# Loading x0 on the ACT queue, with short reads of W1 ahead on the SP queue

## The chip, the cores and the metric

The kernel runs on one core of a Trainium2 chip. The metric is the device time of one execution in microseconds (us). The profile's span, from the first to the last instruction, is about 1.8 us shorter. All quoted runs are of the fast state, or of a kernel that was run once ("unknown"); every profiled run has a mean granted TensorE clock of 1.0 (the share of full clock that the chip allowed). Engines: PE is TensorE, PEld its weight loads, DVE VectorE, ACT ScalarE, POOL GpSimd, SP SyncE. A name ending in q is the engine's issue of transfers.

## The reference, cut to what matters

```python
# x: 1 x 2048 x 640;  W1: 640 x 1536;  bf16
xn = layernorm(x)
out = x + linear_attention(xn, wqkv, wo) + (gelu(xn @ W1 + b1) @ W2 + b2)
```

The argument is about the first 12 us: tile 0 of x (128 tokens, "x0") is loaded, normalised and transposed, and then multiplied with W1. Everything else in the kernel stays as it was.

## The kernel before

All loads of x and W1 are issued by SP, in this order. W1 is 640 x 1536 and comes in four pieces of 384 columns, 480 KB each; a tile of x is 160 KB.

```python
def dma_x(t, n):
    dma("sync", x_in[:, t:t + n, :], ...)
def dma_w1(i):                      # piece i: 384 columns, 5 x 384 elements per partition
    lo, hi = W1P[i]
    dma("sync", W1[:, :, lo:hi], w1v[:, :, lo:hi], [r_W1[i]])

dma_x(0, 1)
dma_x(1, 1)
dma_w1(0)
dma_w1(1)
dma_x(2, 1)
dma_x(3, 1)
dma_w1(2)
...
```

What runs until the first matmul with W1 (cut; `filler` issues dummy matmuls on constants, which keep PE busy until tile 0 is ready):

```python
dma(s_, b1tmp[:], ...)              # b1 on the ACT queue
filler(10)                          # 10 dummies of 512 columns
filler(6, P)                        # 6 of 128 columns
ln_half(0, 0); ln_half(0, 1); ln_aggr(0)      # statistics of tile 0
ln_half(1, 0); ln_half(1, 1)                  # statistics of tile 1
ln_norm(0)                                    # normalise tile 0
transp2(0, b, b + 1)                          # transpose on PE
...
copy2(0, b, b + 1)                            # PSUM to SBUF, ACT and DVE
# order of the first work on W1 ("T1", "T2": transposes of tiles 1 and 2)
plan = h_list(0, 1, 0, 3) + ["T1"] + h_list(0, 1, 3, 6) + h_list(1, 1, 0, 6) + h_list(0, 1, 6, 9)
plan += ["T2"] + ...
```

The first three units (15 matmuls) use W1 piece 0. What follows T1 (60 matmuls) begins with piece 1.

## Time and profile before

| | before |
|---|---|
| time, first 3 runs | 207.79 us (207.78 to 207.91) |
| time, all 39 runs of this study | 207.33 to 208.19 us |
| span of the profiled run | 205.9 us |
| x0 issued, landed | 0.81, 3.20 us |
| first W1 matmul | 6.86 us |
| W1 piece 1 landed | 7.94 us |

Landing times with two decimals are those of the last of a transfer's 16 parts in the trace's records of landings.

From the page of the kernel before, the busy time of PE (us, share of the span, number of instructions; the line goes on with the other engines), and the shares of the engines in the chain that ended last:

```profile
PE 202.7 (98%) x1639; PEld 140.2 (68%) x1639; DVE 109.6 (53%) x227; ACT 74.6 (36%) x153; POOL 35.1 (17%) x85
...
PE 98%; issue 0%; DVE 0%; ACT 0%
```

PE is the whole chain. The chain of waits in order of time (start in us, length in us, what):

```profile
0.84 5.07 PE ps L302 x16
5.91 0.33 PE ps L318 x3
...
6.86 1.00 PE ps L380 x15
...
8.13 3.38 PE ps L380 x60
11.51 0.28 PE ps L361 x5
```

L302 is the dummies, L318 the transposes of tiles 0 and 1, L380 the matmuls with W1, L361 the transposes of tile 2 (T2). The dummies run straight into tile 0's transposes; after 6.86 the chain holds nothing but PE.

From the timeline, SP's issues and DVE's first use of x0 (start, length, engine, line, operation; in brackets idle time and what ended it):

```profile
0.81 0.87 SPq L247 DMA_DIRECT2D xPK<-in_A_x_dram  x2
...
1.73 0.99 SPq L247 DMA_DIRECT2D W<-in_B_w_dram  x2
...
3.23 0.89 DVE L331 BATCH_NORM_STATS2 stats<-xPK 128x6 f32<-128x320 bf16 x2 [3.23 <-DMA xPK<-in_A_x_dram]
```

Each row with x2 is two issues: x0 and x1 from 0.81, W1 pieces 0 and 1 from 1.73. The view of the transfers gives for the issue in progress at 2.3 to 2.45 us, which is W1 piece 1 (number, size, us from issue to landing):

```profile
W<-in_B_w_dram SPq DMA_DIRECT2D x1, 480.0 KB, 5.7
```

Three stretches of time: bounds and length, then busy time of PE, PEld, DVE, ACT, POOL with instruction counts, granted clock, busy share of the DMA engines, and last the GB/s that they moved:

```profile
2.20:3.00 0.80, 0.80 (x4) 0.24 (x3) 0.00 (x0) 0.11 (x1) 0.00 (x0) 1.00 0.98 334
3.20:4.20 1.00, 1.00 (x3) 0.29 (x2) 0.89 (x2) 0.00 (x0) 0.23 (x1) 1.00 0.80 167
4.20:5.00 0.80, 0.80 (x3) 0.29 (x2) 0.78 (x3) 0.00 (x0) 0.49 (x1) 1.00 1.03 348
```

The last column is what to read. While x0 and x1 move it is 334 GB/s; when W1 begins it falls to 167 for a whole microsecond; then it is back at 348.

### The profile page before, as it was taken

The numbers are of one execution on the slowest core, as the hardware profiler recorded it, in microseconds if no ns is written. First come the engines' busy times: TensorE is split into PE (matmuls) and PEld (weight loads), VectorE is DVE, ScalarE is ACT, GpSimd is POOL, SyncE is SP. The second block draws the span as 40 slices with busy tenths as digits, with TensorE's granted clock in tenths as the row PEclk, the third lists the DMA queues.
The fourth block names the chain that finished last, engine by engine and source line by source line (L and its number), as shares of the span: only waits on it lengthen the run. The fifth ranks groups of instructions, "written<-read, shape, count | busy, mean of one in ns | idle before, by whom it ended". The sixth has DMA issues, their size and how long they took to land.

```text
span 205.9 us, 4084 instructions
## 1 busy us (share of the span) xinstructions
PE 202.7 (98%) x1639; PEld 140.2 (68%) x1639; DVE 109.6 (53%) x227; ACT 74.6 (36%) x153; POOL 35.1 (17%) x85
## 2 busy tenths in 40 slices
PE   8999999999999999999999999999999999999995
PEld 2999988544457777777746445677777777777775
DVE  3684288100007888999348888734864322523322
ACT  2699888666676555111153554300000000000000
POOL 3243065800000000999100200000000000000000
PEclk9999999999999999999999999999999999999999
DMA  5958845699910000000000000968611110010011
GB/s 163 348 161 100 241 114 113 132 375 322 360 39 3 0 0 3 0 0 0 3 0 0 2 3 16 357 190 164 159 65 61 36 34 32 33 35 32 32 39 60
DMA packets 24843, 19.70 MB, mean 96 GB/s; under 512 B 9976, under 2 KB 24824, under 8 KB 24824
## 3 DMA queue, kind: packets, MB, share of 16 engines
q1 hardware_dynamic: 23072, 17.86, 29.1%
q10 hardware_dynamic: 1752, 1.58, 4.0%
q8 instruction: 13, 0.21, 0.4%
q14 instruction: 6, 0.05, 0.1%
HBM read 13.11 MB, written 2.62 MB: 76 GB/s over the span
## 4 chain that ended last, share of the span: by engine, by line
PE 98%; issue 0%; DVE 0%; ACT 0%
PE ps L672 36%; PE ps L380 26%; PE ps L489 11%; PE ps L514 11%; PE ps L555 10%; PE ps L302 2%; PE ps L609 1%; PE ps L565 1%; PE ps L619 1%; PE ps L318 0%; DVE W L723 0%; PE ps L361 0%; PE ps L538 0%; ACT b1c L310 0%; ACT xnT L326 0%
## 5 line engine op out<-in xcount | busy, mean ns | idle before, releaser
L672 PE MATMUL ps<-W,HG 128*128 128x320 bf16 (+2 forms) x396 | 54.8, 295 | 0.0
L380 PE MATMUL ps<-xnT,W 128*128 128x128 bf16 (+2 forms) x505 | 53.0, 267 | 0.1
L380 PEld LDWEIGHTS ps<-xnT,W 128*128 128x128 bf16 x505 | 38.4, 98 | 14.1 <-issue 0.3
L672 PEld LDWEIGHTS ps<-W,HG 128*128 128x128 bf16 x396 | 38.1, 98 | 14.5 <-ACT Msb L591 0.2
L384 ACT ACTIVATE HG<-ps,b1c 128x128 bf16<-128x128 f32 (+2 forms) x101 | 42.4, 463 | 11.3 <-PE ps L380 9.3
L683 DVE TENSOR_TENSOR W<-ps,xnT 128x640 bf16<-128x640 f32 x15 | 12.4, 824 | 35.8 <-PE ps L672 34.7
L477 ACT ACTIVATE ek<-ps 128x512 bf16<-128x512 f32 (+1 forms) x36 | 23.2, 644 | 20.4 <-PE ps L555 10.3
L478 DVE TENSOR_SCALAR ek<-ek 128x512 bf16<-128x512 bf16 (+1 forms) x36 | 11.0, 305 | 32.5 <-ACT ek L477 31.3
L672 PE MATMUL ps<-Msb,PQ 128*128 128x320 bf16 (+2 forms) x165 | 24.2, 295 | 0.0
L555 PE MATMUL ps<-xnT,Wqkv 128*128 128x512 bf16 x100 | 21.9, 379 | 0.0
L489 PE MATMUL ps<-Wqkv,xnT 128*128 128x320 bf16 x160 | 21.9, 299 | 0.0
L514 PE MATMUL ps<-xPK,xn_tm 128*128 128x320 bf16 x160 | 21.9, 299 | 0.0
L672 PEld LDWEIGHTS ps<-Msb,PQ 128*128 128x128 bf16 x165 | 15.9, 98 | 5.9
L489 PEld LDWEIGHTS ps<-Wqkv,xnT 128*128 128x128 bf16 x160 | 15.7, 98 | 6.2
L514 PEld LDWEIGHTS ps<-xPK,xn_tm 128*128 128x128 bf16 x160 | 15.7, 98 | 6.1
L508 POOL COPY Wqkv<-Wqkv 128x128 bf16<-128x128 bf16 x25 | 15.1, 603 | 22.9 <-PE ps L489 21.4
L331 DVE BATCH_NORM_STATS2 stats<-xPK 128x6 f32<-128x320 bf16 x32 | 14.0, 477 | 9.3 <-DMA xPK<-in_A_x_dram 9.3
L555 PEld LDWEIGHTS ps<-xnT,Wqkv 128*128 128x128 bf16 x100 | 9.7, 98 | 11.4
L480 DVE SCALAR_TENSOR_TENSOR PQ<-ps,ek 128x512 bf16<-128x512 f32 x20 | 13.8, 692 | 2.1
L480 DVE SCALAR_TENSOR_TENSOR xPK<-ps,ek 128x640 bf16<-128x640 f32 x16 | 13.2, 824 | 1.7
L526 DVE TENSOR_TENSOR Msb<-Msb,xPK 128x640 f32<-128x640 f32 x14 | 11.6, 825 | 0.5
L341 POOL TENSOR_TENSOR rstd<-aggr,mhalf 128x1 f32<-128x1 f32 x16 | 9.9, 620 | 9.0 <-DVE aggr L339 9.0
(57 smaller groups left out, 78.4 us busy)
## 6 DMA issues: line engine op xcount, KB each, us to landing
xnT<-in_A_x_dram SPq DMA_DIRECT2D x4, 640.0 KB, 6.2
Wqkv<-in_A_wqkv_dram SPq DMA_DIRECT2D x3, 800.0 KB, 7.9
out_dram<-W SPq DMA_DIRECT2D x15, 160.0 KB, 1.8
W<-in_B_w_dram SPq DMA_DIRECT2D x4, 480.0 KB, 6.1
W<-in_B_w_dram SPq DMA_DIRECT2D x1, 1920.0 KB, 12.2
xn_tm<-rden ACTq DMA_DIRECT2D x12, 128.0 KB, 3.4
xPK<-in_A_x_dram SPq DMA_DIRECT2D x4, 320.0 KB, 5.3
Wo<-in_A_wo_dram SPq DMA_DIRECT2D x8, 160.0 KB, 8.8
```

Of the source, the lines that this page charges most:

```text
L331: Pl.ins(v, lambda e: e.bn_stats(stats[:, s, 6 * h:6 * h + 6], x_in[:, t, h * HW:(h + 1) * HW]), reads=r_x[t], writes=[r_stats[s][h]])
L380: Pl.ins(pe, [(lambda e, k=k: e.matmul(bank(b, 0, w), W1[:, k, jb * P:(jb + 1) * P], xnT[:, k, tok], start=(k == 0), stop=(k == DT - 1))) ...
L384: Pl.ins(s_, lambda e: e.activation(HG[:, jb, tok], bank(b, 0, w), ACT.Gelu_apprx_tanh, bias=b1c[:, jb:jb + 1]), reads=[B_[b], r_b1c], wri ...
L477: Pl.ins(s_, lambda e: e.activation(e2, src, ACT.Exp), reads=br, writes=[r_ek[s]])
L480: Pl.ins(v, lambda e: e.scalar_tensor_tensor(out=d2, in0=src, scalar=0.0, in1=e2, op0=ALU.max, op1=ALU.add), reads=br + [r_ek[s]], writes= ...
L489: fns.append(lambda e, k=k, h=h, b=b, t=t: e.matmul(bank(b + h, 0, HW), xnT[:, k, t * P:(t + 1) * P], Wqkv[:, k, D + h * HW:D + (h + 1) * ...
L508: Pl.ins(g, lambda e, k=k, i=i: e.tensor_copy(plain(Wqkv[:, k, D:2 * D], i), parts(Wqkv[:, k, 0:D], i)), reads=[r_Wq], writes=[r_Wk, r_WqP])
L514: Pl.ins(pe, [(lambda e, t=t, h=h, b=b, f=f, i=i: e.matmul(bank(b + h, 0, HW), xn_tm[:, t, f * P:(f + 1) * P], PK[:, t, h * HW:(h + 1) * H ...
L526: Pl.ins(v, lambda e, t=t: e.tensor_tensor(out=zsum, in0=zsum, in1=PK[:, t, :], op=ALU.add), reads=[r_PK[t], r_zsum], writes=[r_zsum])
L555: Pl.ins(pe, [(lambda e, k=k, j=j, b=b: e.matmul(bank(b), Wqkv[:, k, D + j * P:D + (j + 1) * P], xnT[:, k, cc], start=(k == 0), stop=(k == ...
L672: Pl.ins(pe, [(lambda e, i=i, x=x, bb=bb: e.matmul(bank(bb, 0, x[1] - x[0]), seq[i][0], seq[i][1][:, x[0]:x[1]], start=(i == 0), stop=(i = ...
L683: Pl.ins(v, lambda e: e.tensor_tensor(out=halves(out_sb[:, s, :]), in0=pair(b), in1=halves(x_res[:, t, :]), op=ALU.add), reads=B_[b:b + 2] ...
```

## The change

W1's start is slow. The intent, as read from the diff, is to touch W1 early with 80 reads of 32 bytes (16 partitions, 5 pieces each, spread over W1), and to move x0 to the other queue so that it doesn't wait behind them.

```diff
+        touch = sb("touch", [16, DT * 16], BF16)
...
-        def dma_x(t, n):
-            dma("sync", x_in[:, t:t + n, :], ...
+        def dma_x(t, n, eng="sync"):
+            dma(eng, x_in[:, t:t + n, :], ...
...
-        dma_x(0, 1)
+        dma("sync", touch[:].rearrange("p (k c) -> p k c", k=DT),
+            w1v.rearrange("(a b) k n -> a b k n", b=P // 16)[:, 0, :, 0:16], [R_("touch")])
+        dma_x(0, 1, s_)
         dma_x(1, 1)
         dma_w1(0)
         dma_w1(1)
```

No instruction of PE, DVE or POOL changes. ACT's table load and its load of b1 come after x0's issue.

More of the change, by code (lines that the diff above doesn't have):

```diff
@@ L250, in dma_t @@
             Pl.ins(eng, lambda e: e.dma_start_transpose(dst, src), reads=reads, writes=writes, dma=True)
-        def dma_x(t, n):
-            dma("sync", x_in[:, t:t + n, :], xv[t * P:(t + n) * P, :].rearrange("(t p) d -> p t d", p=P),
+        def dma_x(t, n, eng="sync"):
+            dma(eng, x_in[:, t:t + n, :], xv[t * P:(t + n) * P, :].rearrange("(t p) d -> p t d", p=P),
                 sum(r_x[t:t + n], []))
```

## The prediction

> **What bounds the kernel.** TensorE: the page gives PE 98% busy of a 205.9 us span at granted clock 1.0, and the chain of waits is PE from end to end. The list of waits has no wait of PE for a DMA; after its first W1 matmul at 6.86 us PE never idles. Only what moves that 6.86, or opens a gap after it, moves the time (207.79 us).
>
> **The start (timeline, 0 to 8 us).** SP issues x0 at 0.81; it lands 2.4 us later, at 3.2, and DVE's first statistics start (3.23). Then rstd on POOL (to 5.08) and normalisation of tile 0 from 5.20; its first part ends near 5.57. PE meanwhile runs 16 dummy matmuls from 0.84: ten of 512 columns, 0.43 us apart, six of 128, about 0.11 apart, so to about 5.7. The transposes start at 5.71. So dummies and tile 0 finish together: an earlier x0 gains nothing, a later x0 costs its delay nearly one for one. Then ACT copy 6.27 to 6.76, W1 matmuls at 6.86.
>
> **What the change aims at.** Windows of 0.2 us show 295 to 358 GB/s while x0 and x1 move (2.2 to 3.0), only 54, 108, 161, 230 GB/s from 3.2 to 4.0 when W1 begins, and over 330 from 4.2. Against 340 GB/s about 200 KB are missing, some 0.6 us. The 80 short reads over W1 seem meant to take this slow first contact early, with x0 on the ACT queue so as not to wait behind them.
>
> **What it is worth.** W1 piece 0 (issued 1.73, landing 4.7 us later) is there at 6.4, wanted at 6.86; piece 1 (2.2 + 5.7) at 7.9, wanted near 8.0; piece 2 (3.81 + 6.5) at 10.3, wanted near 10.5. All tight but in time: having them 0.3 to 0.6 us earlier gives PE nothing. Gain on the chain: about 0.
>
> **What it costs.**
> - SP issues the short reads in x0's slot, about 0.43 us either way; x1 and W1 keep their issue times within 0.1 us. x1 (landing 3.55, wanted 4.35) has 0.8 us to spare.
> - ACT issues x0 before its table load (1.28 us) and b1 (issue 0.62 us); both have over 2 us of slack. x0's issue comes 0 to 0.15 us later than SP's.
> - The Trainium skill, "DMA: Bandwidth & Descriptors", section "Issuing engines are not separate DMA queues", says transfers of different issuing engines interleave on the same 16 DMA engines; no run here shows it yet. So x0 shares with the short reads, which may hold an engine during their slow first contact, and with x1. I estimate x0 landing 0.1 to 0.6 us later (3.3 to 3.8 us).
>
> Sum: 0 gained, 0.05 to 0.5 us lost at the start, most likely near 0.15.
>
> **Prediction: 207.95 us, range 207.5 to 208.5; faster by over 2%: 0.01, within 2%: 0.98, slower by over 2%: 0.01.**
>
> **What would show it.**
> - The slow stretch at W1's start shrinks or moves ahead of x1; W1 piece 0 lands 0.2 to 0.6 us earlier.
> - DVE's first statistics start at 3.3 to 3.8; the first transpose and first W1 matmul come later by the same less about 0.05. The end moves by that alone.
> - PE still never waits for DMA after its first W1 matmul.
>
> **What would make it wrong.** If the dummies end earlier (PE reaches full clock at another moment), the start could gain 0.1 to 0.2 us. If the short reads hold x1 and W1 behind them, pieces 1 and 2, with 0.1 to 0.2 us of slack, become PE waits and the loss reaches 1 us. If x1 slips over 0.8 us, it delays tile 0's normalisation, which follows x1's statistics on DVE.

## The result

| | before | after |
|---|---|---|
| time, same rounds | 207.83 us (207.75 to 207.91, 6 runs) | 207.91 us (207.66 to 208.27, 6 runs) |
| ratio, after over before | | 1.0004, 95% interval 0.9991 to 1.0017 |
| once more, later | 207.65 us (207.43 to 207.83, 11 runs) | 207.53 us (207.43 to 207.90, 5 runs) |
| ratio | | 1.0001, interval 0.9988 to 1.0014 |

A ratio is the mean time of one kernel's fast runs over that of the other's of the same rounds, so it is not quite the ratio of the medians. The change does nothing that these runs can tell from zero.

The profile after, in the same views. The page's first line:

```profile
PE 203.0 (98%) x1639; PEld 140.1 (68%) x1639; DVE 109.6 (53%) x227; ACT 74.7 (36%) x153; POOL 35.1 (17%) x85
```

The chain of waits (three lines were added to the file, so L305, L321, L383, L364 are the dummies, the transposes of tiles 0 and 1, the W1 matmuls, and T2):

```profile
0.84 5.06 PE ps L305 x16
5.91 0.53 PE ps L321 x5
...
6.92 1.00 PE ps L383 x15
...
8.21 3.52 PE ps L383 x60
11.74 0.28 PE ps L364 x5
```

The timeline's issues, and DVE's first use of x0:

```profile
0.81 0.40 SPq L248 DMA_DIRECT2D touch<-in_B_w_dram  x1
...
0.82 0.42 ACTq L248 DMA_DIRECT2D xPK<-in_A_x_dram  x1
...
1.26 0.41 SPq L248 DMA_DIRECT2D xPK<-in_A_x_dram  x1
...
1.72 1.02 SPq L248 DMA_DIRECT2D W<-in_B_w_dram  x2
...
3.20 0.89 DVE L334 BATCH_NORM_STATS2 stats<-xPK 128x6 f32<-128x320 bf16 x2 [3.20 <-DMA xPK<-in_A_x_dram]
```

W1 piece 1, from issue to landing:

```profile
W<-in_B_w_dram SPq DMA_DIRECT2D x1, 480.0 KB, 6.0
```

The three stretches:

```profile
2.20:3.00 0.80, 0.80 (x4) 0.24 (x3) 0.00 (x0) 0.56 (x2) 0.00 (x0) 1.00 0.89 302
3.20:4.20 1.00, 1.00 (x3) 0.29 (x2) 0.89 (x3) 0.00 (x0) 0.23 (x1) 1.00 0.70 171
4.20:5.00 0.80, 0.80 (x3) 0.29 (x2) 0.80 (x3) 0.00 (x0) 0.52 (x1) 1.00 1.09 359
```

From the list of waits (who waited for what: us in total, times, longest), the one wait of PE's weight loads for W1:

```profile
PEld ps L383 <- DMA W<-in_B_w_dram: 0.2, 1, 0.2
```

The reader should see four things. x0 is not late: DVE starts on it at 3.20 against 3.23, although ACT issues it. The short reads take x0's slot on SP (0.40 us), so x1 and W1 keep their issue times (1.26, 1.72). The slow microsecond is still there, 171 GB/s against 167. And this trace is 0.23 us longer at T2 (11.74 against 11.51): 0.06 us at the first W1 matmul and the rest where PE waits at 8.21 for W1 piece 1, which landed at 8.17.

### One sum that fits every trace

A reading that all the experiments use, with their traces already in the table. The matmuls after T2 are the same in all kernels here, and PE does them without a gap that differs: span minus the start of T2 is between 194.4 and 194.5 us in all fourteen traces. So everything happens before T2, and there two things compete:

- from the first W1 matmul to T2 takes 4.63 us if nothing waits (6.90 to 11.53 in the run touch_wide below);
- from the landing of W1 piece 1 to T2 takes 3.57 us (8.17 to 11.74 in the trace after).

T2 starts at the later of the two:

| trace | x0 landed | first W1 matmul | W1 piece 1 landed | later of (matmul + 4.63, piece 1 + 3.57) | T2 measured | span |
|---|---|---|---|---|---|---|
| before | 3.20 | 6.86 | 7.94 | 11.51 | 11.51 | 205.9 |
| after | 3.17 | 6.92 | 8.17 | 11.74 | 11.74 | 206.2 |
| after_again | 3.18 | 6.62 | 7.76 | 11.33 | 11.33 | 205.8 |
| act_only | 3.79 | 7.24 | 7.44 | 11.87 | 11.87 | 206.3 |
| touch_only | 3.54 | 6.98 | 8.23 | 11.80 | 11.80 | 206.2 |
| touch_wide | 3.25 | 6.90 | 7.76 | 11.53 | 11.53 | 206.0 |
| spacer | 3.19 | 7.02 | 8.40 | 11.97 | 11.97 | 206.4 |
| wait_only | 3.08 | 6.57 | 7.73 | 11.30 | 11.29 | 205.7 |
| x1_act | 3.27 | 7.80 | 7.30 | 12.43 | 12.43 | 206.9 |
| eight_dummies | 3.26 | 6.70 | 7.67 | 11.33 | 11.32 | 205.8 |
| eight_again | 3.18 | 6.63 | 7.69 | 11.26 | 11.26 | 205.7 |
| after_eight | 3.15 | 6.76 | 7.86 | 11.43 | 11.43 | 205.9 |
| w2_touch | 3.30 | 6.92 | 8.31 | 11.88 | 11.88 | 206.3 |
| w2_split | 3.14 | 6.82 | 8.26 | 11.83 | 11.83 | 206.3 |

The two constants are read from touch_wide and after; the other twelve traces follow within 0.01 us. The sum is still a description. It is useful because it says for each run what set the time: what comes before the first W1 matmul (x0, x1, the dummies or piece 0), or W1 piece 1. In nine of the fourteen traces, the kernel before among them, it is piece 1 (in eight_again the two are equal).

### The profile page after: what moved, and what is told of

It is laid out like the page before. It is cut to its first block, busy times and chain, and to the rows that moved or that the text cites. A ratio compares the mean times of both kernels' runs of the same rounds, so it can differ in the third digit from the quotient of the medians.

```text
span 206.2 us, 4085 instructions
## 1 busy us (share of the span) xinstructions
PE 203.0 (98%) x1639; PEld 140.1 (68%) x1639; DVE 109.6 (53%) x227; ACT 74.7 (36%) x153; POOL 35.1 (17%) x85
## 4 chain that ended last, share of the span: by engine, by line
PE 98%; DVE 0%; issue 0%
PE ps L675 36%; PE ps L383 26%; PE ps L517 11%; PE ps L492 11%; PE ps L558 10%; PE ps L305 3%; PE ps L612 1%; PE ps L568 1%; PE ps L622 1%; PE ps L321 0%; DVE W L726 0%; PE ps L364 0%; PE ps L541 0%; PE ps L311 0%
## 5 line engine op out<-in xcount | busy, mean ns | idle before, releaser
L383 PE MATMUL ps<-xnT,W 128*128 128x128 bf16 (+2 forms) x505 | 53.0, 267 | 0.1
L383 PEld LDWEIGHTS ps<-xnT,W 128*128 128x128 bf16 x505 | 38.4, 98 | 14.2 <-DMA W<-in_B_w_dram 0.2
```

The lines of the kernel that those rows point to most:

```text
L383: Pl.ins(pe, [(lambda e, k=k: e.matmul(bank(b, 0, w), W1[:, k, jb * P:(jb + 1) * P], xnT[:, k, tok], start=(k == 0), stop=(k == DT - 1))) ...
```

## The experiments

Theories at the start. A: W1's slow microsecond is how a long load with several pieces per partition starts, so touching W1 can't help. B: it is first contact with W1's memory, and the short reads soften it. S came after the first four runs: the short reads are worth only the time for which they hold x1 back. C: what scatters is the moment at which PE reaches full clock, seen through the dummies.

### The two halves alone, and the change once more

act_only is the changed kernel without the short reads:

```diff
-        dma("sync", touch[:]..., w1v...[:, 0, :, 0:16], [R_("touch")])
         dma_x(0, 1, s_)
```

> Half of the change: x0 on the ACT queue, no short reads. SP then issues x1 at 0.81 us and W1 piece 0 at about 1.27, 0.45 us earlier than before. Theory A (the slow stretch at W1's start is how a long load with several pieces per partition starts, engine after engine): the stretch keeps its depth and its length of about 1 us but begins up to 0.4 us earlier, W1 piece 1 lands at 7.5 to 7.8 instead of 7.9 to 8.2, PE has no wait for W1, 207.7 to 207.8 us. Theory B (the stretch is first contact with W1's memory, and the short reads soften it): the stretch is deeper than with the short reads, and W1 lands no earlier than 7.9. In either case the time is within 0.15% of before, because x0 lands at 3.2 and PE's dummy matmuls run to 5.7.

Measured: 208.14 us (208.03 to 208.18, 5 runs), ratio to before 1.0023 (1.0011 to 1.0035). Both theories had said "within 0.15% of before, because x0 lands at 3.2", and both missed. Timeline and chain of this run:

```profile
0.81 0.40 SPq L247 DMA_DIRECT2D xPK<-in_A_x_dram  x1
...
0.82 0.41 ACTq L247 DMA_DIRECT2D xPK<-in_A_x_dram  x1
...
3.81 0.89 DVE L331 BATCH_NORM_STATS2 stats<-xPK 128x6 f32<-128x320 bf16 x2 [3.81 <-DMA xPK<-in_A_x_dram]
```

```profile
0.82 2.97 DMA xPK<-in_A_x_dram
...
6.22 0.36 PE ps L318 x3
...
7.24 1.00 PE ps L380 x15
...
11.87 0.28 PE ps L361 x5
```

x0 is issued as early as ever, but x1 is now issued in the same moment on the other queue. The trace's packets show the two interleaved: x1's first and last packet start at 1.83 and 3.18 us, x0's at 2.11 and 3.39; in the kernel before, x0's are at 1.85 and 2.59, and x1's follow from 2.59. So x0 lands at 3.79 instead of 3.20, the chain now begins with x0's transfer (2.97 us of it), and the first W1 matmul comes at 7.24. This agrees with the Trainium skill, "DMA: Bandwidth & Descriptors", section "Issuing engines are not separate DMA queues": transfers from different engines share the same 16 DMA engines and interleave. In return W1 landed early (piece 1 at 7.44), which bought nothing, as x0 was later still.

touch_only is the other half:

```diff
-        dma_x(0, 1, s_)
+        dma_x(0, 1)
```

> The other half: short reads first, x0 on SP behind them. Both theories: x0 is issued at 1.25 and lands at 3.6 instead of 3.2, x1 at 3.9 to 4.0, first transpose at 6.0 to 6.1 instead of 5.7, first W1 matmul at 7.1 to 7.2 instead of 6.86. W1 piece 0 is issued at 2.2 and lands 0.3 to 0.5 later (6.8 to 6.9), piece 1 at 8.3 to 8.6, close to its use at 8.3. Time 208.1 to 208.6 us. Were PE's start not set by x0, the time would stay at 207.8.

Measured: 207.93 us median; five runs from 207.74 to 207.96 and one of 210.04, which makes the ratio 1.003 (1.0001 to 1.0059). That run alone has a mean granted clock of 0.992; the other five average 207.89 us, 0.25 above before. The median is below the expected 208.1 to 208.6. x0 landed at 3.54, and the first W1 matmul came at 6.98, less late than expected. W1 piece 1 landed at 8.23 and set the time. In this half too x0's delay reaches the first W1 matmul, only smaller.

> The changed kernel once more, for a second trace and the scatter of its times. If the PE wait of 0.2 us for W1 piece 1 comes from the change, it is there again and piece 1 lands at 8.1 to 8.3; if it was chance (one DMA engine late), piece 1 lands anywhere from 7.8 to 8.3 and the time follows it. Median 207.7 to 208.0, spread again over 0.4 us, which is more than the 0.16 of before.

Measured: 207.53 us (207.43 to 207.90), ratio 1.0001. W1 piece 1 landed at 7.76 instead of 8.17 in the same program. So the wait of 0.2 us in the first trace need not come from the change. In the table, w2_touch and w2_split load x and W1 exactly as the kernel before does, and piece 1 landed at 8.31 and 8.26 there: the lateness is a lottery that both kernels play. The landing records show how: in the trace of before, 15 of the 16 parts of piece 0 landed between 5.17 and 5.76 us and the last at 6.46, and in piece 1 one part is 0.7 us behind again.

### Do the short reads prepare W1?

touch_wide reads 32 bytes of every row of W1, 640 reads instead of 80:

```diff
-        touch = sb("touch", [16, DT * 16], BF16)
+        touch = sb("touch", [P, DT * 16], BF16)
-            w1v.rearrange("(a b) k n -> a b k n", b=P // 16)[:, 0, :, 0:16], [R_("touch")])
+            w1v[:, :, 0:16], [R_("touch")])
```

> The short reads on all 128 partitions: 640 of 32 bytes, every row of W1[...]. Theory B (first contact with W1's memory, the 80 reads being too few or on the wrong engines): the slow stretch after x1 vanishes (over 250 GB/s in all windows of 0.2 us from 3.2 to 4.2) and W1 piece 1 lands at 7.6 or earlier. Theory A (start-up of a long load with several pieces per partition): the stretch stays, and the short reads, being such a load themselves, take 0.5 to 1 us more and delay x1 and W1 by as much; W1 piece 1 lands after 8.2, time 207.9 to 208.6.

Measured: 207.86 us (207.68 to 208.06), ratio 1.0012 (1.0000 to 1.0024). The microsecond from 3.2 stayed slow, at 145 GB/s, which speaks against B, though these reads landed only at 3.48, when W1 had already begun. x1 landed at 4.64 and held up tile 0's normalisation, which comes after x1's statistics on DVE. W1 piece 1 landed at 7.76: neither "7.6 or earlier" (B) nor "after 8.2" (A).

spacer turns the 80 short reads to Wqkv, which nothing needs before 40 us:

```diff
-            w1v.rearrange("(a b) k n -> a b k n", b=P // 16)[:, 0, :, 0:16], [R_("touch")])
+            wqv.rearrange("(a b) k n -> a b k n", b=P // 16)[:, 0, :, 0:16], [R_("touch")])
```

> The changed kernel with its 80 short reads turned to Wqkv, which nothing needs before 40 us: same shape, same place in SP's queue, no contact with W1. Theory S (the short reads are worth only the 0.45 us by which they hold back x1's issue, so that x0 has the DMA engines to itself): as the changed kernel: x0 lands at 3.1 to 3.3 against 3.8 with x0 on ACT and no short reads, W1 piece 1 at 7.7 to 8.3, time 0.2 to 0.6 us below that kernel's, 207.5 to 208.0. Theory B (they prepare W1's memory): W1 piece 0 or 1 lands 0.3 us or more later than in the two traces of the changed kernel (6.4; 7.8 and 8.2), and the time is 208.1 or more.

Measured: 207.81 us (207.57 to 208.14), ratio 1.0004 (0.9988 to 1.0021), the same ratio as the change itself. x0 landed at 3.19. The profiled run was one of the slower ones, and its chain shows why:

```profile
2.21 6.19 DMA W<-in_B_w_dram
...
8.45 3.52 PE ps L383 x60
11.97 0.28 PE ps L364 x5
```

Here W1 piece 1 is the chain (2.21 to 8.40 us). Piece 0 came late too (6.98), as theory B expected of this run; but w2_split, without any short reads, had piece 0 at 6.78 and w2_touch at 6.87, so a single landing doesn't tell the theories apart. The times do, and they go against B.

wait_only has no short reads at all. SP waits for a memset of POOL, which was there anyway and ends near 1.2 us, before it issues x1:

```diff
+        dma_x(0, 1, s_)
+        Pl.ins(g, ...memset(onesm[:], 1.0)...)      # the three memsets moved up,
+        Pl.ins(g, ...memset(ident[:], 0.0)...)      # mhalf's now last
+        Pl.ins(g, ...memset(mhalf[:], -0.5)...)
+        Pl.wait_event("sync", r_small.w)            # mhalf's memset is done
         dma_x(1, 1)
```

> x0 on the ACT queue with no short reads at all; instead SP waits for a small POOL memset (done near 1.2 us) before it issues x1, so x1 and W1 keep the issue times of the changed kernel (1.27, 1.72) and nothing stands in their place. Theory S (the short reads only hold x1 back by 0.45 us): x0 lands at 3.1 to 3.3 as in the changed kernel, not at 3.8; time 207.4 to 208.0, 0.2 to 0.6 us below x0 on ACT alone. Theory B (they help by what they read): like x0 on ACT alone, 208.0 to 208.2.

Measured: 207.54 us (207.48 to 207.71), ratio 0.9992 (0.9979 to 1.0005). Its timeline:

```profile
0.81 0.39 ACTq L247 DMA_DIRECT2D xPK<-in_A_x_dram  x1
...
1.21 0.40 SPq L247 DMA_DIRECT2D xPK<-in_A_x_dram  x1
...
1.67 0.98 SPq L247 DMA_DIRECT2D W<-in_B_w_dram  x2
...
3.10 0.89 DVE L332 BATCH_NORM_STATS2 stats<-xPK 128x6 f32<-128x320 bf16 x2 [3.10 <-DMA xPK<-in_A_x_dram]
```

x1 is issued at 1.21 instead of 0.81, and x0 is in use at 3.10 instead of 3.81. Against act_only, whose ratio is 1.0023, that is 0.6 us gained by a wait (and a new order of three memsets). With spacer this settles S: what the short reads read doesn't matter, they hold x1, and W1 behind it, back long enough for x0 to go first. It also rules out that the ACT queue is slower in itself: x0 landed at 3.08 through it. In the kernel before, SP's own order did the same for nothing.

x1_act turns the order round: x0 alone and first on SP, W1 right behind it, x1 on the ACT queue after b1:

```diff
         dma_x(0, 1)
-        dma_x(1, 1)
         dma_w1(0)
...
         dma(s_, b1tmp[:], B_b1.rearrange("(a p) -> a p", p=P), [r_b1tmp])
+        dma_x(1, 1, s_)
```

> The other way round: x0 first on SP and alone, W1 piece 0 right behind it (issued at 1.25 instead of 1.73), x1 on the ACT queue behind b1 (issued near 1.5). Theory S: x0 lands at 3.2 as before, x1 at 3.7 to 4.3 (wanted at 4.3), W1 piece 0 at 5.4 to 6.2 instead of 6.4, piece 1 at 7.2 to 7.8 instead of 7.9; PE never waits for W1; time as before or up to 0.2 us lower, with less scatter. If W1's start holds back whatever shares the engines with it, x1 lands after 4.4 and tile 0's normalisation slips; the time rises by that, 0.1 to 0.5 us.

Measured: 209.67 us (208.59 to 210.68), ratio 1.0095 (1.0062 to 1.0128), the worst of all. Two things are mixed in it. Three runs (208.59, 208.87, 209.01) have a granted clock of 1.0, and their mean is 1.1 us above that of before (207.68). The other three (210.33 to 210.68) have 0.992. As PE is busy 98% of the time, I estimate that 0.8% of the clock costs 0.8% of 209 us, 1.7 us, and the means of the two groups do differ by 1.65. Why the clock was lower there is not shown. The chain of the profiled run, one of the first three:

```profile
1.54 4.00 DMA xPK<-in_A_x_dram
...
7.80 1.00 PE ps L379 x15
```

x1 took 4.00 us from issue to landing, against 2.3 in the kernel before. The packets show none of x1 before 3.94 us, while 316 packets of W1 had started by then; those of b1, ahead of x1 on the same queue, had all started by 2.70. Tile 0's normalisation, behind x1's statistics on DVE, then came about 1.2 us late. In theory S's terms: a load on the second queue was not only slowed by what the first queue held, here it also started late. Why it started that late was not tested.

### Where does W1's slow microsecond come from?

A slow stretch of the same kind comes at 47 us, where PE doesn't depend on the loads. The next two experiments, and their expectations, took it for the start of W2's load. The landings say otherwise, as told after w2_split, so neither run tests what it was made for. The views are stretches of time as above; the kernel before first, ahead of the slow stretch, in it, and where W2 does begin:

```profile
46.00:47.00 1.00, 1.00 (x7) 0.43 (x5) 0.00 (x0) 0.69 (x1) 0.00 (x0) 1.00 1.07 367
47.25:48.25 1.00, 1.00 (x7) 0.41 (x5) 0.00 (x0) 0.61 (x2) 0.00 (x0) 1.00 0.71 175
51.75:52.75 1.00, 1.00 (x6) 0.44 (x5) 0.00 (x0) 0.61 (x2) 0.00 (x0) 1.00 1.08 373
```

w2_touch puts short reads of every row of W2 in front of Wqkv (issued at 38.99 us, landed at 41.84):

```diff
+        dma("sync", touch[:].rearrange("p (k c) -> p k c", k=JT),
+            B_w2.rearrange("(k p) n -> p k n", p=P)[:, :, 0:16], [R_("touch")])
         dma("sync", Wqkv[:, :, D:2 * D], wqv[:, :, D:2 * D], [r_Wk])
```

> Kernel before, with short reads of every row of W2 (1536 of 32 bytes) ahead of Wqkv, some 8 us before W2 itself is loaded; PE needs none of it before 126 us, so the time stays at 207.6 to 207.9. Before, W2's load began with five windows of 0.25 us at 154 to 231 GB/s (47.25 to 48.5) after 350 and more. Theory A (start of a long load with many pieces per partition): the slow stretch after Wo is there again, about 1.2 us at 150 to 250 GB/s. Theory B (first contact): it is gone, over 320 GB/s throughout.

The slow stretch now begins near 48.5:

```profile
48.50:49.50 1.00, 0.95 (x6) 0.41 (x6) 0.00 (x0) 0.69 (x1) 0.00 (x0) 1.00 0.74 120
```

120 GB/s: the stretch came later with the whole queue and is not softened. (The one time, 208.04 us, has W1 piece 1 at 8.31.) w2_split loads W2 by 12 transfers of one piece per partition, like Wo:

```diff
-        dma("sync", W2[:], B_w2.rearrange("(k p) n -> p k n", p=P), [r_W2])
+        for k in range(JT):
+            dma("sync", W2[:, k, :], B_w2[k * P:(k + 1) * P, :], [r_W2k[k]])
```

> Kernel before with W2 loaded by 12 transfers of one piece per partition (as Wo is) instead of one with 12 pieces per partition; the same bytes, first contact at the same moment. PE doesn't need W2 before 126 us, time as before. Theory A (slow start of a load with many pieces per partition): no window of 0.25 us under 300 GB/s between Wo and the middle of W2. Theory B (first contact with W2's memory): the slow stretch of about 1.2 us at 100 to 230 GB/s is there in spite of the split.

```profile
46.00:47.00 1.00, 1.00 (x6) 0.47 (x5) 0.00 (x0) 0.61 (x2) 0.00 (x0) 1.00 1.03 361
47.25:48.25 1.00, 1.00 (x6) 0.48 (x5) 0.00 (x0) 0.69 (x1) 0.00 (x0) 1.00 0.67 202
```

202 GB/s instead of 175: the slow stretch stays in spite of the split. (The one time, 208.03 us, has W1 piece 1 at 8.26.)

But W2 isn't in it. In this trace, where each piece of W2 has its own landing record, the first part of W2's first piece landed at 51.89 us. The first parts of the loads ahead of it in SP's queue landed at 47.37 (Wqkv's third and last piece), 47.82 (b2, one row of 1280 bytes read into all 128 partitions) and 48.19 to 51.46 (Wo's eight pieces). In the kernel before it is 47.18, 47.61 and 48.02 to 51.19. So the slow stretch lies between the end of Wqkv and the first pieces of Wo, with b2's load in the middle; whether that load causes it was not tested. W2 begins between 51 and 53 us, and from 49.5 to 56 us no quarter of a microsecond is under 317 GB/s in any of the three traces. So W2, with 12 pieces per partition and nothing read of it before, has no slow start at all in the kernel before, and the two runs say nothing for or against A or B at W1.

What is left for W1: short reads ahead don't remove its slow microsecond (171 and 145 GB/s), and the same load isn't always slow. In act_only, where W1 was issued 0.45 us earlier and began while x0 and x1 were still moving, the microsecond from 3.2 ran at 326 GB/s without any short reads. Theory A had expected the stretch there with the same depth and length, up to 0.4 us earlier, but no 0.2 us from 2.6 to 4.4 is under 290 GB/s in that trace; in that form it fails too. What causes the slow microsecond stays open. A reading that no run tests: W1 had its first packet 1.3 us after its issue in the kernel before (1.73, 3.00), whereas W2 had been waiting in the queue for almost 5 us (issued at 46.37).

### The dummies

eight_dummies is the kernel before with two dummies fewer:

```diff
-        filler(10)
+        filler(8)
```

> The kernel before with 8 instead of 10 wide dummy matmuls. Theory C (what is left of the scatter, 206.6 to 206.9 us for the first W1 matmul in traces of like kernels, is the moment at which PE reaches full clock, 5.3 to 6.6 us, which sets the end of the dummies): they end at 4.9 or earlier, the transposes start when tile 0 is normalised (5.55 to 5.65) in every run, the first W1 matmul at 6.6 to 6.75, time 0.05 to 0.25 us lower with less scatter. If dummies aren't what PE's start waits for, no change. If fewer dummies leave PE at half clock for longer, it is slower by up to 0.3.

(The expectation's "206.6 to 206.9 us for the first W1 matmul" is a slip for 6.6 to 6.9.) Measured: 207.52 us (207.41 to 207.58), ratio 0.9992 (0.9978 to 1.0005). The chain no longer begins with the dummies:

```profile
0.81 2.45 DMA xPK<-in_A_x_dram
...
5.68 0.35 PE ps L318 x3
...
6.70 1.00 PE ps L380 x15
```

x0's transfer is the head of the chain now, and the first W1 matmul came at 6.70 instead of 6.86. eight_again is the same kernel once more, after_eight the change with 8 dummies.

> The kernel before with 8 wide dummies once more, to see whether its small gain (ratio 0.9992, interval across 1) and its narrow scatter (0.17 us) hold: 207.4 to 207.6, 0.05 to 0.25 us below before. If it was chance, it is equal to before within 0.05 us.

> The changed kernel with 8 instead of 10 wide dummy matmuls. Theory C (dummies at half clock hide or show the start by chance; what remains is W1 piece 1's lateness): first W1 matmul at 6.6 to 6.7 in every run, 207.4 to 207.8 us, the rest of the scatter from W1 piece 1 landing after 8.0. If the change were worth something that the dummies hid, it beats the 8-dummy kernel without the change by over 0.1 us; I expect within 0.1.

Measured: eight_again 207.74 us, four runs from 207.42 to 207.78 and two at 209.12 and 209.21, ratio 1.0019 (0.9990 to 1.0047). after_eight 208.45 us, three runs from 207.48 to 207.91 and three from 208.98 to 209.16, ratio 1.0038 (1.0010 to 1.0066). Both expectations missed, and the small gain of eight_dummies doesn't hold: with fewer dummies some runs take 1.5 us more. None of the profiled runs is one of these, so their cause is not shown. A guess: the clock of PE. Dummies of 128 columns are 0.11 us apart at the start, W1 matmuls of 128 columns 0.056 (60 in 3.35 us), so PE starts at half speed. The granted clock of the five slower runs is given as 1.0, but that figure leaves out the time before the first full clock (before has 1.0 too), so a late start wouldn't show in it. The trace's clock record puts the moment of full clock at 6.11 us in before, 6.60 in after, 5.29 in after_again, 5.49 in wait_only, and 4.58, 5.65 and 6.29 in the three traces with 8 dummies (act_only and spacer have no such record; their wide dummies go from 0.43 to 0.22 us apart near 4.0 us). The Trainium skill, "TensorE: Matmul & The Clock Gate", section "What's actually happening", says that the activity window of 3.4 us is free-running and isn't reset by the kernel's start, which agrees with this scatter; a PE left idle before tile 0 could then miss a window. Against the guess stands act_only, where PE is idle for 1.2 us before the transposes and no run of five jumped; in its trace full clock had come before the idle time.

Nothing here beats the kernel before clearly. wait_only is the best candidate, with an interval that includes 1.

## Why the prediction was right or wrong

- **The time.** Predicted 207.95 us in 207.5 to 208.5, "within 2%" at 0.98. Measured 207.91. Right, though the most likely loss of 0.15 us is not confirmed: the ratios 1.0004 and 1.0001 are worth 0.08 and 0.02 us, both inside the noise. The range also holds the time of a change that does nothing (207.83), so the number can't tell a right account from a wrong one. It came out right although the loss it was built on, a late x0, didn't happen: in that it was lucky.
- **"PE from end to end", "only what moves that 6.86, or opens a gap after it".** Right. It is the sum of the table above: after T2 all traces agree within 0.1 us, and a gap after the first W1 matmul is what piece 1 opens in nine of them.
- **"So dummies and tile 0 finish together: an earlier x0 gains nothing, a later x0 costs its delay nearly one for one."** Right but for 0.2 us. The chains of before and after begin with the dummies; with two fewer, the chain begins with x0. In four of the traces whose chain runs through x0 (act_only, touch_only, eight_dummies, eight_again), the first W1 matmul comes 3.44 or 3.45 us after x0's landing (in after_eight, with full clock only at 6.29, 3.61). For before that would be 6.64, not 6.86: there the dummies, and transposes still at half clock, would have hidden the first 0.22 us of a delay. In act_only x0 was 0.6 us later, and the first W1 matmul came 0.38 later than before and 0.62 later than in after_again, the trace of the changed kernel in which full clock came early.
- **"I estimate x0 landing 0.1 to 0.6 us later."** Wrong for the change: 3.17 against 3.20. This is the step that failed. The sharing is real, act_only shows it at its full 0.6 us, but the short reads themselves prevent it, as they occupy SP's first slot for 0.40 us and x1 comes after them. I had counted that slot only as neutral for x1 and W1.
- **The short reads "may hold an engine during their slow first contact".** Not seen; x0 was unharmed, and the reads landed at 2.71, 1.9 us after their issue.
- **"W1 piece 0 lands 0.2 to 0.6 us earlier", "The slow stretch at W1's start shrinks or moves ahead of x1".** Wrong: 6.44 against 6.46, and 171 against 167 GB/s. The intent of the change failed at its first step.
- **"Having them 0.3 to 0.6 us earlier gives PE nothing."** Right to 0.02 us for the trace it was read from (11.49 against 11.51 in the sum), but not in general. In w2_touch and w2_split, with the same loads, piece 1 cost 0.33 and 0.38 us (the difference of the two terms). One trace showed slack where the next showed a wait.
- **"PE still never waits for DMA."** Wrong in the first trace after (0.2 us). This was in the list of what could go wrong, as a result of slow short reads; the experiments show it happens without them too.
- **"If the dummies end earlier (PE reaches full clock at another moment)."** It did move by chance: the first W1 matmul is at 6.92 in one trace of the changed kernel and at 6.62 in the next.

Where did the intended gain go? It was never made: the short reads don't make W1 faster. The change consists of a loss (x0 on the second queue, 0.45 to 0.5 us alone) and a repair of it (short reads of W1 or of Wqkv or a plain wait, each of which delays x1 by 0.4 us), and the sum is the old schedule.

## What to carry to other kernels

Here a second queue gave no second set of engines: moving the urgent load to the free queue put it in competition with what the first queue issued in that moment (x0 at 3.79 us), whereas one queue in the right order let it go first (3.20). When two halves of a change cancel, undo each alone, and replace the one that seems to help by a plain wait of the same length. Before calling a load "in time", look at its landing in several traces; here W1 piece 1, loaded in the same way, landed at 7.94 in one and at 8.31 in another. And before naming the load that a slow stretch belongs to, look at the landings: what this study took for W2's start was b2 and Wo.

## What the Trainium skill lacked or had wrong

- "DMA: Bandwidth & Descriptors", section "Issuing engines are not separate DMA queues", has the sharing right and names saved issue time as the only gain of a second issuing engine. It lacks the price for the first of two loads: issued together on two queues they landed at 3.60 and 3.79 us, issued 0.4 us apart on one queue at 3.20 and 3.53.
- The same page, section "Queues, rings and completion order", says that each DMA engine alternates between the queues at the granularity of packets. In x1_act a load issued at 1.54 on the ACT queue had no packet before 3.94, while 316 packets of the SP queue started. The page doesn't say when a second queue's load may start so late; the cause was not found here.
- No page has the slow start of W1: from 3.2 us about 1 us at 82 to 172 GB/s in twelve of the fourteen traces (249 in x1_act, 326 in act_only), with 334 and 348 around it in the kernel before. It outlives short reads of W1 in advance (103 to 172).
- No page has a time for how far one of the 16 parts of a load lags: 0.7 us behind the next slowest in the trace before (6.46 against 5.76), and the same again in the next piece (7.94 against 7.24).
- "TensorE: Matmul & The Clock Gate", section "What's actually happening", gives about 0.5 us either way for the moment of full clock. In these traces, with PE's start always at 0.84, it ranged from 4.58 to 6.60 us by the clock record, and was near 4.0 by the dummies' spacing in act_only and spacer.
